# Chunk-selected attention and squared-ReLU FFN: batch-wide loads, first batch by query blocks, values and ones in one stationary, value products four steps late

## The chip, the cores and the metric

One core of one Trainium2 chip. The metric is the device time of one execution, in microseconds (us), median of the runs. Times of the kernel before scatter between 375 and 382 us (one run fell to 369.5). The granted TensorE clock, averaged over a run, lies between 0.96 and 1.00, because in most executions it falls to half for a short stretch or two; this explains only part of the scatter, as runs at 0.995 took 381 us too, and the one of 369.5 us was at 1.00. Engines: PE is TensorE (matmul), PEld its weight load, DVE VectorE, ACT ScalarE, POOL GpSimd.

## The reference

Batch 4, 8 heads, 768 positions, head dimension 64. Keys are grouped in chunks of 32; each query may attend only to the 6 chunks whose upper bound on the score is highest. The attention output then passes through a squared-ReLU FFN.

```python
k_min, k_max = per-chunk min and max of k                 # 24 chunks of 32 keys
ub = sum_d max(q*k_min, q*k_max)                          # masked causally by chunk
top_chunks = argsort(ub)[..., -6:]
scores = where(chunk selected and key <= query, q @ k.T / 8, -1e9)
attn_out = softmax(scores) @ v
x = attn_out as (3072 tokens, 512)
out = relu(x @ w_in)**2 @ w_out                           # 512 -> 2048 -> 512
```

## The kernel before

Two heads (a "pair") are handled together; a batch has four pairs. **Stage A** of a pair transposes k and q (`kT`, `qT`), takes chunk minima and maxima on DVE, computes the bound (`ub`), selects with MAX8 and transposes the selection (`sT`) into extra rows of q. **Stage B** computes scores, exp and value products for two query blocks of 384. The **FFN** of a 384-token block is 28 units of matmul work (16 "up", 12 "down") that fill TensorE between attention steps.

```python
# stage B, kernel before, cut
av  = psav.tile([128, QB], F32, tag="av")     # numerators of both heads, 64 rows each
den = psav.tile([128, QB], F32, tag="den")    # denominators, in another PSUM tile
def values(j):                                # called one key step after the scores
    for hh in range(2):
        rows = slice(D*hh, D*hh + D)
        matmul(av[rows, off:],  lhsT=vn[:, hh, j, :], rhs=e[:, off:], ...)   # 64 wide
        matmul(den[rows, off:], lhsT=ones,            rhs=e[:, off:], ...)   # 64 wide
...
nc.scalar.activation(rc, den, ACT.Ln)                     # the "finish"
nc.scalar.activation(rc, rc, ACT.Exp, scale=-1.0)
nc.vector.tensor_mul(xT[:, hp, cols], av, rc)
# ... order of the work
for p in range(B * NP):                       # pair by pair
    stage_a(p + 1); stage_b(p, [1, 2])        # [1, 2]: FFN units per key step
    if hp == NP - 1:                          # batch done: release two FFN blocks
        ...
```

The softmax here doesn't subtract the row's maximum and nothing guards it: scores larger than these inputs give would overflow.

Of the kernel before, what the change touches and what calls it, by code (L numbers as in the profile page):

```python
# [18 lines left out]
def kernel(  # L19
# [32 lines left out]
    ld = ctx.enter_context(tc.tile_pool(name="ld", bufs=3))  # L52
    work = ctx.enter_context(tc.tile_pool(name="work", bufs=2))
    epool = ctx.enter_context(tc.tile_pool(name="epool", bufs=6))
    hpool = ctx.enter_context(tc.tile_pool(name="hpool", bufs=2 * NFI))
    opool = ctx.enter_context(tc.tile_pool(name="opool", bufs=3))
    pst = ctx.enter_context(tc.tile_pool(name="pst", bufs=2, space=PSUM))
    pss = ctx.enter_context(tc.tile_pool(name="pss", bufs=2, space=PSUM))
# [3 lines left out]
    def load_qk(p):  # L62
        b, hp = divmod(p, NP)
        st = {}
        for nm, src in (("k", k), ("q", q)):
            t = ld.tile([128, 2, NT, D], BF16, tag=nm + "n", name=nm + "n")
            nc.gpsimd.dma_start(  # L67
                out=t, in_=src[b, 2 * hp:2 * hp + 2].rearrange(
                    "h (p j) d -> p h j d", p=128))
            st[nm] = t  # L70
        return st

    def load_v(p):
        b, hp = divmod(p, NP)
        t = ld.tile([128, 2, NT, D], BF16, tag="vn", name="vn")
        nc.gpsimd.dma_start(  # L76
            out=t, in_=v[b, 2 * hp:2 * hp + 2].rearrange(
                "h (j p) d -> p h j d", p=128))
        return t

    states = {0: load_qk(0)}

    ident = consts.tile([128, 128], BF16, tag="ident")
    make_identity(nc, ident)
    ones = consts.tile([128, D], BF16, tag="ones")
    nc.vector.memset(ones, 1.0)

    states[0]["v"] = load_v(0)
    states[1] = load_qk(1)
    states[1]["v"] = load_v(1)  # L90

    onehot = consts.tile([NC, S], BF16, tag="onehot")
    nc.gpsimd.memset(onehot, 0.0)
    nc.gpsimd.affine_select(
        out=onehot, in_=onehot,
        compare_op=ALU.not_equal, fill=NEG,
        base=0, channel_multiplier=1,
        pattern=[[-1, NC], [0, CH]],
    )
# [3 lines left out]
    ubmask = consts.tile([128, NS, 2, NC], F32, tag="ubmask")  # L103
    nc.gpsimd.memset(ubmask, 0.0)
    for g in range(4):
        nc.gpsimd.affine_select(
            out=ubmask[g * 32:(g + 1) * 32],
            in_=ubmask[g * 32:(g + 1) * 32],
            compare_op=ALU.is_ge, fill=-1e9,
            base=4 + g, channel_multiplier=0,  # L110
            pattern=[[4, NS], [0, 2], [-1, NC]],
        )


    NSET = 2
    kq, qs, kmx, kmn, selb = [], [], [], [], []
    for s in range(NSET):
        for hh in range(2):
            t = consts.tile([KC, S], BF16, tag=f"kq{s}{hh}", name="kqc")
            nc.scalar.copy(t[D:KC, :], onehot)  # L120
            kq.append(t)
            t = consts.tile([KC, S], BF16, tag=f"qs{s}{hh}", name="qsc")
            nc.vector.memset(t[D:KC, 0:128], 0.0)
            qs.append(t)
        for lst, nm in ((kmx, "kmx"), (kmn, "kmn")):
            t = consts.tile([128, 2, NC], BF16, tag=f"{nm}{s}", name=nm)
            nc.vector.memset(t, 0.0)
            lst.append(t)
        t = consts.tile([128, NS, 2, 32], BF16, tag=f"selb{s}", name="selb")
        nc.gpsimd.memset(t, 0.0)  # L130
        selb.append(t)
# [5 lines left out]
    def load_weights():  # L137
        nc.gpsimd.dma_start(
            out=w_in_sb, in_=moe_w_in.rearrange("(ki p) f -> p ki f", p=128))
        nc.gpsimd.dma_start(  # L140
            out=w_out_sb, in_=moe_w_out.rearrange("(fi p) d -> p fi d", p=128))

    def stage_a(p):

        st = states[p]
        s = p % NSET
        for nm in ("k", "q"):
            pt = pst.tile([128, S], BF16, tag="tp", name=nm + "T")
            n = st[nm]
            for j in range(NT):  # L150
                for hh in range(2):
                    nc.tensor.matmul(pt[D * hh:D * hh + D, 128 * j:128 * (j + 1)],  # L152
                                     lhsT=n[:, hh, j, :], rhs=ident,
                                     is_transpose=True,
                                     start=(j == 0), stop=(j == NT - 1))
            tt = work.tile([128, S], BF16, tag=nm + "t", name=nm + "t")
            nc.vector.tensor_copy(tt.rearrange("d (p j) -> d p j", j=NT),  # L157
                                  pt.rearrange("d (j p) -> d p j", j=NT))
            if nm == "k":
                for op, dst in ((ALU.max, kmx[s]), (ALU.min, kmn[s])):  # L160
                    for hh in range(2):
                        rows = slice(D * hh, D * hh + D)
                        nc.vector.tensor_reduce(  # L163
                            dst[rows, hh, :],
                            tt[rows].rearrange("d (c j) -> d c j", j=CH),
                            axis=AX.X, op=op)
                comb = kq
            else:
                qp = work.tile([128, S], BF16, tag="qp", name="qp")
                nc.vector.tensor_scalar_max(qp[:, 128:], tt[:, 128:], 0.0)  # L170
                qm = work.tile([128, S], BF16, tag="qm", name="qm")
                nc.vector.tensor_scalar_min(qm[:, 128:], tt[:, 128:], 0.0)
                comb = qs
            for hh in range(2):
                nc.vector.tensor_copy(comb[2 * s + hh][0:D, :],
                                      tt[D * hh:D * hh + D, :])
        ub = pst.tile([128, NS, 2, NC], F32, tag="tp", name="ub")
        for i in range(NS):
            cols = slice(128 * (i + 1), 128 * (i + 2))
            nc.tensor.matmul(ub[:, i], lhsT=qp[:, cols], rhs=kmx[s],  # L180
                             start=True, stop=False)
            nc.tensor.matmul(ub[:, i], lhsT=qm[:, cols], rhs=kmn[s],
                             start=False, stop=True)
        ubm = work.tile([128, NS, 2, NC], F32, tag="ubm", name="ubm")
        nc.vector.tensor_add(ubm, ub, ubmask)
        m8 = work.tile([128, NS, 2, 8], F32, tag="m8", name="m8")
        for i in range(NS):
            for hh in range(2):
                nc.vector.max(out=m8[:, i, hh], in_=ubm[:, i, hh])
        nc.vector.tensor_tensor(  # L190
            selb[s][:, :, :, 0:NC], ubm,
            m8[:, :, :, TOPK - 1:TOPK].to_broadcast([128, NS, 2, NC]),
            op=ALU.is_lt)
        sT = pst.tile([64, S], BF16, tag="tp", name="sT")
        for i in range(NS):
            nc.tensor.matmul(sT[:, 128 * (i + 1):128 * (i + 2)],  # L196
                             lhsT=selb[s][:, i], rhs=ident, is_transpose=True,
                             start=(i == 0), stop=(i == NS - 1))
        for hh in range(2):
            nc.vector.tensor_copy(qs[2 * s + hh][D:KC, 128:],  # L200
                                  sT[32 * hh:32 * hh + NC, 128:])

    ffn = []

# [39 lines left out]
    def run_ffn(n):  # L244
        for _ in range(min(n, len(ffn))):
            ffn.pop(0)()

    def stage_b(p, per_step):

        b, hp = divmod(p, NP)  # L250
        st = states.pop(p)
        s = p % NSET
        vn = st["v"]
        for blk in range(NBLK):
            q0, q1 = QB * blk, QB * (blk + 1)
            av = psav.tile([128, QB], F32, tag="av", name="av")
            den = psav.tile([128, QB], F32, tag="den", name="den")
            nj = q1 // 128
            es = {}

            def values(j):
                off = max(0, 128 * j - q0)
                for hh in range(2):
                    rows = slice(D * hh, D * hh + D)
                    e = es.pop((j, hh))
                    nc.tensor.matmul(av[rows, off:], lhsT=vn[:, hh, j, :],  # L266
                                     rhs=e[:, off:],
                                     start=(j == 0), stop=(j == nj - 1))
                    nc.tensor.matmul(den[rows, off:], lhsT=ones,  # L269
                                     rhs=e[:, off:],  # L270
                                     start=(j == 0), stop=(j == nj - 1))

            for j in range(nj):
                off = max(0, 128 * j - q0)
                for hh in range(2):
                    ps = pss.tile([128, QB], F32, tag="ps", name="ps")
                    nc.tensor.matmul(  # L277
                        ps[:, off:],
                        lhsT=kq[2 * s + hh][:, 128 * j:128 * (j + 1)],
# [11 lines left out]
                if j > 0:  # L291
                    values(j - 1)
# [9 lines left out]
    for p in range(B * NP):  # L302
# [4 lines left out]
        if p == 1:  # L307
            load_weights()
# [38 lines left out]
```

## Time and profile before

| | kernel before |
|---|---|
| time, median of the first three runs | 376.87 us (374.68 to 381.01) |
| span of the profiled execution | 379.1 us |
| busy: PE, DVE, ACT | 347.6, 219.0, 207.3 us |
| first 100 us / 100 to 330 us: PE busy | 79.2 / 223.1 us |

From the page of the kernel before: the line of busy times (us, share of the span, instructions), four rows of the span in 40 slices (tenths busy; PEclk is the granted clock in tenths), and the two lines of the chain of work that ended last.

```profile
PE 347.6 (92%) x2367; PEld 163.3 (43%) x2384; DVE 219.0 (58%) x585; ACT 207.3 (55%) x509; POOL 100.7 (27%) x257
...
PE   1298998799899999999999999999999999999996
...
DVE  3894548837777486817684677709592953041230
ACT  2253546645565477545765576447664777462541
...
PEclk9999999957999999999999999999999999999999
...
PE 75%; POOL 9%; issue 5%; ACT 5%; DMA 4%; DVE 1%; POOLq 0%; ACTq 0%
PE ph L213 22%; PE py L227 21%; PE ps L277 10%; PE av L266 9%; PE den L269 8%; DMA w_in_sb<-in_moe_w_in_dram 4%; POOL e L286 2%; POOL vn L76 2%; POOL qn L67 2%; ACT e L283 2%; PE sT L196 2%; POOL kn L67 1%; ACT rc L298 1%; PE kT L152 1%; PE qT L152 1%
```

Three quarters of the chain lie on TensorE; DVE and ACT together have 6%. A page of matmul busy time must be read with care: a busy PE is not a PE at its peak. So I use a second measure throughout, **streaming time**: each matmul counted as its moving columns at 2.4 per ns, plus 2.5 ns (which gives the 0.162 and 0.216 us at which FFN matmuls of 384 and 512 columns start after one another at the end); 64-wide neighbours that start nearer together than that count their measured distance. It is an estimate from the trace of the least TensorE time that the work needs. **The rest** is span minus streaming time: waiting, slow clock, weight loads that did not overlap. (17 down matmuls missing in this trace are added at 0.216 us.) Before: first 100 us, streaming 39, rest 61; after that, streaming 233, rest 46.

Table of windows, kernel before; after the window and its length come PE, PEld, DVE, ACT and POOL busy (us, instructions), granted clock, DMA share, GB/s:

```profile
0.00:100.00 100.00, 79.18 (x505) 34.78 (x506) 64.49 (x162) 46.99 (x112) 42.42 (x96) 0.93 0.71 92
100.00:330.00 230.00, 223.06 (x1630) 105.91 (x1645) 142.51 (x391) 140.39 (x358) 58.27 (x161) 1.00 0.26 39
```

The same kind of table for instructions on the FFN's first half alone (`ph`; columns: PE and ACT busy, clock, DMA share, GB/s), kernel before:

```profile
50.00:90.00 40.00, 5.71 (x13) 1.47 (x3) 0.83 0.35 34
90.00:106.00 16.00, 6.76 (x30) 3.43 (x7) 1.00 0.27 30
106.00:140.00 34.00, 7.99 (x41) 5.30 (x11) 1.00 0.40 59
140.00:160.00 20.00, 8.87 (x44) 5.42 (x11) 1.00 0.29 31
```

FFN work arrives in earnest after about 82 us. One caution on the clock column: no clock was recorded before 56 us here, and the views count that time as 1.00. The matmuls say otherwise: 384-column scores take about 0.50 us until 55 us, and 0.33 right after.

Timeline of TensorE, kernel before (start, duration, instruction, count): one key step's four value matmuls, and elsewhere a pair of them.

```profile
174.71 0.32 PE L266 MATMUL av<-e,vn 128*64 128x384 bf16 x1 [0.19 <-POOL e L286]
174.87 0.32 PE L269 MATMUL den<-e,ones 128*64 128x384 bf16 x1
174.96 0.32 PE L266 MATMUL av<-e,vn 128*64 128x384 bf16 x1
175.12 0.32 PE L269 MATMUL den<-e,ones 128*64 128x384 bf16 x1
...
201.20 0.35 PE L269 MATMUL den<-e,ones 128*64 128x384 bf16 x2
```

In the first four lines two starts come 0.16 us after the one before, serial, and one 0.09.

### The profile page before, as it was taken

The page shows a single profiled execution, that of the slowest core. Times are in us where ns is not written, and L with a number is a line of the kernel's source. Part 1 is how long each engine was busy: PE and PEld are TensorE (multiplying, and loading weights), DVE is VectorE, ACT ScalarE, POOL GpSimd, SP SyncE. Part 2 cuts the span into 40 slices and gives each one's busy share as a digit, 9 for nine tenths or more (in the row PEclk, how much of TensorE's full clock was granted, in tenths as well). Part 3 has the DMA queues.
Part 4 walks back from the last instruction along what each step waited for, and adds up shares of the span by engine and source line. Part 5 has one row for each costly group of instructions (what it writes and reads, how often), then busy time and mean ns, then how long its engine had stood idle before and what let it go on. Part 6 is the DMA issues. An engine that isn't in the chain of part 4 may idle for free.

```text
span 379.1 us, 6701 instructions
## 1 busy us (share of the span) xinstructions
PE 347.6 (92%) x2367; PEld 163.3 (43%) x2384; DVE 219.0 (58%) x585; ACT 207.3 (55%) x509; POOL 100.7 (27%) x257
## 2 busy tenths in 40 slices
PE   1298998799899999999999999999999999999996
PEld 1234243334354454444444445444544544454552
DVE  3894548837777486817684677709592953041230
ACT  2253546645565477545765576447664777462541
POOL 8623442514050505023140415021221121100000
PEclk9999999957999999999999999999999999999999
DMA  9999924606051423217060606040031000100102
GB/s 105 115 214 202 144 16 48 64 0 64 1 53 39 58 61 30 35 57 91 2 62 29 90 30 63 1 79 29 2 21 57 28 3 0 58 28 29 55 1 83
DMA packets 39617, 20.35 MB, mean 54 GB/s; under 512 B 25760, under 2 KB 36000, under 8 KB 39584
## 3 DMA queue, kind: packets, MB, share of 16 engines
q0 software_dynamic: 36128, 13.63, 31.0%
q1 hardware_dynamic: 3456, 6.29, 4.3%
q8 instruction: 18, 0.29, 0.3%
q14 instruction: 15, 0.12, 0.1%
HBM read 27.26 MB, written 6.29 MB: 89 GB/s over the span
## 4 chain that ended last, share of the span: by engine, by line
PE 75%; POOL 9%; issue 5%; ACT 5%; DMA 4%; DVE 1%; POOLq 0%; ACTq 0%
PE ph L213 22%; PE py L227 21%; PE ps L277 10%; PE av L266 9%; PE den L269 8%; DMA w_in_sb<-in_moe_w_in_dram 4%; POOL e L286 2%; POOL vn L76 2%; POOL qn L67 2%; ACT e L283 2%; PE sT L196 2%; POOL kn L67 1%; ACT rc L298 1%; PE kT L152 1%; PE qT L152 1%
## 5 line engine op out<-in xcount | busy, mean ns | idle before, releaser
L283 ACT ACTIVATE e<-ps 128x384 bf16<-128x384 f32 (+2 forms) x288 | 110.2, 420 | 63.1 <-PE ps L277 49.7
L286 POOL TENSOR_SCALAR_AFFINE_SELECT e<-e 128x128 bf16<-128x128 bf16 x192 | 55.0, 298 | 208.6 <-ACT e L283 206.5
L213 PE MATMUL ph<-xT,w_in_sb 128*128 128x384 bf16 x512 | 103.9, 332 | 2.3 <-ACT ht L218 1.3
L218 ACT ACTIVATE ht<-ph 128x384 bf16<-128x384 f32 x128 | 62.6, 492 | 39.1 <-PE ph L213 35.5
L277 PE MATMUL ps<-qsc,kqc 88*128 88x384 bf16 (+2 forms) x288 | 76.3, 313 | 4.0 <-ACT e L283 2.9
L269 PE MATMUL den<-e,ones 128*64 128x384 bf16 (+2 forms) x288 | 67.9, 320 | 0.1
L213 PEld LDWEIGHTS <-w_in_sb 128*128 128x128 bf16 x512 | 45.5, 98 | 46.6 <-issue 20.0
L266 PE MATMUL av<-e,vn 128*64 128x384 bf16 (+2 forms) x288 | 59.2, 331 | 5.4 <-POOL e L286 3.8
L277 PEld LDWEIGHTS <-kqc 88*128 88x128 bf16 x288 | 25.9, 99 | 32.0 <-issue 17.1
L232 ACT COPY ob<-py 128x512 f32<-128x512 f32 x24 | 14.0, 584 | 44.5 <-PE py L227 44.5
L269 PEld LDWEIGHTS <-ones 128*64 128x64 bf16 x288 | 25.1, 114 | 27.9 <-issue 23.3
L299 DVE TENSOR_TENSOR xT<-av,rc 128x384 bf16<-128x384 f32 x32 | 17.6, 550 | 30.2 <-ACT rc L298 29.1
L266 PEld LDWEIGHTS <-vn 128*64 128x64 bf16 x288 | 19.8, 113 | 34.4 <-issue 30.8
L157 DVE COPY kt<-kT 128x768 bf16<-128x768 bf16 x16 | 15.3, 956 | 29.2 <-PE kT L152 29.0
L163 DVE TENSOR_REDUCE kmn<-kt 64x24 bf16<-64x768 bf16 x32 | 30.3, 947 | 0.4
L163 DVE TENSOR_REDUCE kmx<-kt 64x24 bf16<-64x768 bf16 x32 | 30.1, 942 | 0.3
L200 DVE COPY qsc<-sT 24x640 bf16<-24x640 bf16 x32 | 15.5, 484 | 17.1 <-PE sT L196 16.6
L297 ACT ACTIVATE rc<-den 128x384 f32<-128x384 f32 x32 | 15.7, 491 | 14.1 <-PE den L269 14.1
L76 POOL DMA_DIRECT2D vn<-in_v_dram x16 | 16.6, 1039 | 12.6 <-PE den L269 9.2
L298 ACT ACTIVATE rc<-rc 128x384 f32<-128x384 f32 x32 | 16.8, 523 | 0.4
L152 PE MATMUL kT<-ident,kn 128*64 128x128 bf16 x192 | 12.2, 250 | 5.0 <-DMA kn<-in_k_dram 5.0
L157 DVE COPY qt<-qT 128x768 bf16<-128x768 bf16 x16 | 15.2, 948 | 0.9 <-PE qT L152 0.9
(451 smaller groups left out, 388.1 us busy)
## 6 DMA issues: line engine op xcount, KB each, us to landing
out_dram<-ob SPq DMA_DIRECT2D x24, 256.0 KB, 2.0
kn<-in_k_dram POOLq DMA_DIRECT2D x16, 192.0 KB, 4.5
qn<-in_q_dram POOLq DMA_DIRECT2D x16, 192.0 KB, 4.6
vn<-in_v_dram POOLq DMA_DIRECT2D x16, 192.0 KB, 4.2
w_in_sb<-in_moe_w_in_dram POOLq DMA_DIRECT2D x1, 2048.0 KB, 15.8
w_out_sb<-in_moe_w_out_dram POOLq DMA_DIRECT2D x1, 2048.0 KB, 18.9
```

The costliest lines, as they stand in the source:

```text
L76: nc.gpsimd.dma_start(out=t, in_=v[b, 2 * hp:2 * hp + 2].rearrange("h (j p) d -> p h j d", p=128))
L157: nc.vector.tensor_copy(tt.rearrange("d (p j) -> d p j", j=NT), pt.rearrange("d (j p) -> d p j", j=NT))
L163: nc.vector.tensor_reduce(dst[rows, hh, :], tt[rows].rearrange("d (c j) -> d c j", j=CH), axis=AX.X, op=op)
L213: nc.tensor.matmul(ph, lhsT=w_in_sb[:, ki, 128 * f:128 * (f + 1)], rhs=xT[:, ki, t0:t0 + QB], start=(ki == 0), stop=(ki == NKI - 1))
L218: nc.scalar.activation(ht, ph, ACT.Relu)
L227: nc.tensor.matmul(py, lhsT=h2[f][:, 128 * t:128 * (t + 1)], rhs=w_out_sb[:, f, :], start=(f == 0), stop=(f == NFI - 1))
L266: nc.tensor.matmul(av[rows, off:], lhsT=vn[:, hh, j, :], rhs=e[:, off:], start=(j == 0), stop=(j == nj - 1))
L269: nc.tensor.matmul(den[rows, off:], lhsT=ones, rhs=e[:, off:], start=(j == 0), stop=(j == nj - 1))
L277: nc.tensor.matmul(ps[:, off:], lhsT=kq[2 * s + hh][:, 128 * j:128 * (j + 1)], rhs=qs[2 * s + hh][:, q0 + off:q1], start=True, stop=True)
L283: nc.scalar.activation(e[:, off:], ps[:, off:], ACT.Exp, scale=scale)
L286: nc.gpsimd.affine_select(out=e[:, off:off + 128], in_=e[:, off:off + 128], compare_op=ALU.is_ge, fill=0.0, base=0, channel_multiplier=-1, ...
L298: nc.scalar.activation(rc, rc, ACT.Exp, scale=-1.0)
```

## The change

Its intent: fewer, larger loads; start FFN work early by running the first batch block by block; halve the value matmuls by putting values and ones side by side in one 128-wide stationary; keep masks and exp off TensorE's path by diagonal keys first and a lag of four steps. It also moves q's copies out of PSUM to ACT, reduces k over 128 rows at once, and spreads FFN units by an even rate. The core of the diff, with cuts:

```diff
-    pst = tc.tile_pool(name="pst", bufs=2, PSUM)      # transposes, ub, sT
-    pss = tc.tile_pool(name="pss", bufs=2, PSUM)      # scores
+    pst = tc.tile_pool(name="pst", bufs=1, PSUM)
+    pss = tc.tile_pool(name="pss", bufs=3, PSUM)
...  # stage A
-            nc.vector.tensor_copy(tt, pt)             # q: one 128-row copy, then two of 64
+                    nc.scalar.copy(qs[s][hh][0:D, cols], by_token[D*hh:D*hh+D])
-                        nc.vector.tensor_reduce(dst[rows, hh, :], tt[rows], ...)  # 64 rows
+                nc.vector.tensor_reduce(kr[:, m], kt, axis=AX.X, op=op)          # 128 rows
...  # stage B
-                    nc.tensor.matmul(av[rows, off:], lhsT=vn[:, hh, j, :], ...)
-                    nc.tensor.matmul(den[rows, off:], lhsT=ones, ...)
+                c0 = 2*D*(NT*(2*hp + hh) + j) - D*hh   # [v|1] for head 0, [1|v] for head 1
+                nc.tensor.matmul(av[hh][:, off:],
+                    lhsT=vo[b % 2].rearrange("p h n d -> p (h n d)")[:, c0:c0 + 2*D], ...)
...  # finish
-            nc.scalar.activation(rc, den, ACT.Ln)
+            for hh in range(2):
+                nc.scalar.activation(rc[D*hh:D*hh+D],
+                    av[hh][D*(1-hh):D*(1-hh)+D], ACT.Ln)
             nc.scalar.activation(rc, rc, ACT.Exp, scale=-1.0)
-            nc.vector.tensor_mul(xT[:, hp, cols], av, rc)
+            for hh in range(2):
+                rows = slice(D*hh, D*hh + D)
+                nc.vector.tensor_mul(xT[rows, hp, cols], av[hh][rows], rc[rows])
...  # order
+    LAG = 4
+    order = list(range(nj - HT, nj)) + list(range(nj - HT))    # diagonal keys first
+    A  = [(p, (half,)) for half in range(2) for p in range(NP)]     # batch 0 by halves
+    Bk = [(p, blk) for blk in range(NBLK) for p in range(NP)]       # batch 0 by blocks
+    # batches 1 and 2 pair by pair, batch 3 by blocks
+    pace["rate"] = (n_tok // QB - 1) * nunits / tot_cols            # one FFN rate
```

## The prediction

> **What bounds the kernel now.** From 100 to 330 us TensorE: the table of windows has it busy 223 of 230 us (DVE 143, ACT 140), and the chain of waits alternates FFN lines with score and value matmuls. A batch takes about 82.5 us there (first long py stretch at 115.7, 199.0, 280.5); 43 of it is FFN (a pure FFN block takes 21.5 us at the end). Before 100 us it is latency: the columns streamed there need 46 us at full clock but took 96. The first batch has no FFN work to fill with and is paced by one pair's serial chain on DVE (kt copy 0.96 us, four reductions of 0.95), by POOL's DMA issues, and by a slow array: 384-column score matmuls last 0.50 us up to about 55 us and again at 77 to 90, else 0.33. The Trainium skill (TensorE: Matmul & The Clock Gate, Part 1) says that activity releases a half-rate clock; the profile's 0.50 slice agrees.
>
> **What changes.**
> 1. Value products: four 64-wide matmuls per key block, which in the timeline start 0.16, 0.09, 0.16, 0.16 us apart at 384 columns, 0.57 us in all (the skill's Part 3, on column tiling, says halves of the array can overlap; the 0.09 shows it for one pair). After: two 128-wide, 0.32 us. 112 such steps' worth of columns x 0.25 = 28 us of TensorE time, nearly all critical.
> 2. Switches from 64-wide den to a full-width matmul lose about 0.1 us each (82 into FFN: 8.8 us excess); values four steps late no longer wait for exp and mask (7 us excess after scores). Estimated gain 9 us.
> 3. First batch by query blocks: FFN block 0 can begin after four short block-0 attentions and w_in's landing, near 30 to 37 us instead of about 100. That fills TensorE and warms its clock: estimated gain 25 to 35 us. Against it: a single transpose buffer serialises stage A, w_out is queued late, and twelve one-hot copies of 0.82 us precede ACT's first q copies.
> 4. Side engines: 128-row reductions save DVE 30 us, removed q copies 26; divided xT products and qp/qm cost about 28. ACT gains q copies (26), second Ln (16), one-hots (7): 207 to about 255 us, 80% of the new span, the nearest rival of TensorE.
>
> **Sum.** 377 - 28 (values) - 9 (switches) - 29 (start) + 3 (ACT queueing, transpose buffer) = 314. From below: attention 27 + FFN 43 = 70 us per batch instead of 82.5; 35 us start + 248 mixed + 21.5 last FFN block + 5 to 10 stalls = 310 to 315.
>
> **Predicted: 314 us, 298 to 336. Faster by over 2%: 0.96; within 2%: 0.03; slower: 0.01.**
>
> **What would show it.** Two value matmuls per step 0.16 us apart; batch period near 70 us; ph in earnest before 40 us, and 384-column matmuls at 0.33 us from then on; a pure FFN tail of one block, not two; ACT busy 245 to 260, DVE 190 to 205.
>
> **What would make it wrong.** ACT as limiter (batch period over 75, TensorE waiting on exp or on the av buffer behind Ln and Exp): 325 to 340. First batch stalled on DMA (w_out, second-half loads), clock cold to 60 us or more: 325 to 335. If neither binds: 298 to 305.

## More of the kernel before

A compile-time scheduler orders each engine's instructions; each engine then runs its own list in that order.

Of the 368 places where two value matmuls are neighbours in this trace, 176 overlap by more than half.

The finish of one block, kernel before, all engines:

```profile
261.37 0.49 ACT L297 ACTIVATE rc<-den 128x384 f32<-128x384 f32 x1 [0.80 <-PE den L269]
262.12 0.52 ACT L298 ACTIVATE rc<-rc 128x384 f32<-128x384 f32 x1
262.54 0.35 PE L269 MATMUL den<-e,ones 128*64 128x384 bf16 x1
...
265.98 0.55 DVE L299 TENSOR_TENSOR xT<-av,rc 128x384 bf16<-128x384 f32 x1
267.34 0.52 PE L266 MATMUL av<-e,vn 128*64 128x384 bf16 x4
```

`den` is free as soon as Ln has read it, so the next block's denominators begin at 262.54, over 3 us before the numerators of the old block are released by the product at 265.98. They serve as filler. Afterwards four numerator matmuls catch up in 0.52 us.

## The result

| | before | after |
|---|---|---|
| time, median (range), 4 runs each | 378.94 us (374.68 to 381.37) | 358.93 us (357.79 to 359.95) |
| ratio of fast runs | | 0.9551 (0.948 to 0.962) |
| span of the profiled execution | 379.1 | 357.3 |
| streaming time, first 100 us / later | 39 / 233 | 49 / 210 |
| the rest, first 100 us / later | 61 / 46 | 51 / 47 |

A ratio is the mean time of a kernel's fast runs over that of the other's fast runs of the same rounds, so not quite the ratio of the medians. Executions over 1.5% slower than the fastest of the same kernel are left out of the means. As the runs of before fall on both sides of the line between fast and slow, ratios of different groups are not exactly alike either; below I compare medians, and the before of each group (378.1 to 380.8 us) moved by under 1%.

The change is faster by 4.5%, not by 17%. The time lies far outside my range. TensorE's matmuls fell about as I had asked for; what the chain of work consists of is another thing. The page of the kernel after, same lines as before:

```profile
PE 308.7 (86%) x2096; PEld 160.0 (45%) x2096; DVE 218.6 (61%) x678; ACT 253.3 (71%) x589; POOL 96.7 (27%) x243
...
PE   0276689999789998789999999999799999999996
...
DVE  7688779747958766769482868379991331250320
ACT  6665568955968865977957897778749996671541
...
PEclk9999999999969999959999999999999999999999
...
PE 57%; ACT 20%; DVE 17%; issue 4%; POOL 1%; ACTq 0%; POOLq 0%; DVEq 0%
PE ph L256 19%; PE py L270 16%; PE ps L346 7%; ACT e L350 5%; ACT rc L328 4%; ACT kqc L121 2%; ACT qsc L177 2%; PE kT L170 2%; ACT rc L331 2%; DVE qp L209 2%; DVE kr L187 2%; ACT ht L261 2%; DVE xT L334 2%; PE qT L170 2%; DVE kt L183 2%
```

The share of DVE and ACT in the chain went from 6% to 37%. TensorE has less to do and is idle for longer (span less busy time: 31.5 us before, 48.6 after), although the rest fell from 107 to 98 us. PEclk shows two dips (a 6 and a 5 in the row; the clock records put them at 99.9 to 106.8 and 151.1 to 161.4 us, both at half).

Windows of the kernel after, columns as before:

```profile
0.00:100.00 100.00, 71.30 (x505) 35.51 (x506) 75.58 (x258) 70.28 (x160) 45.36 (x97) 1.00 0.98 118
100.00:330.00 230.00, 213.74 (x1471) 112.82 (x1470) 137.32 (x406) 172.84 (x409) 51.33 (x147) 0.96 0.19 31
```

And for `ph` alone:

```profile
50.00:90.00 40.00, 12.26 (x56) 7.92 (x16) 1.00 0.54 64
90.00:106.00 16.00, 4.11 (x13) 0.87 (x2) 0.81 0.82 67
106.00:140.00 34.00, 11.42 (x53) 6.92 (x14) 0.99 0.36 51
140.00:160.00 20.00, 1.81 (x6) 0.00 (x0) 0.78 0.21 35
```

FFN work begins in earnest at 53 us (29 us earlier than the 82 of the kernel before, but not at 30 to 37 as I said). The first block's 28 units are used up by 89 us, and the second's input is complete only at 102. The second's units are used up by 140; from 140 to 160 us there are 1.8 us of it where before had 8.9, and the clock falls in just these holes (0.81 and 0.78). So work was brought forward and then was missing. The last value product is at 308.5 us; 49 us of pure FFN follow, more than two blocks, where I had promised one.

The finish of one block in the kernel after, all engines:

```profile
188.41 0.33 PE L314 MATMUL av_2681<-e,vo 128*128 128x384 bf16 x1
188.61 0.49 ACT L328 ACTIVATE rc<-av_2680 64x384 f32<-64x384 f32 x1 [0.54 <-PE av_2680 L314]
189.13 0.48 ACT L328 ACTIVATE rc<-av_2681 64x384 f32<-64x384 f32 x1
189.91 0.51 ACT L331 ACTIVATE rc<-rc 128x384 f32<-128x384 f32 x1
190.46 0.55 DVE L334 TENSOR_TENSOR xT<-av_2680,rc 64x384 bf16<-64x384 f32 x1 [2.49 <-ACT rc L331]
191.04 0.56 DVE L334 TENSOR_TENSOR xT<-av_2681,rc 64x384 bf16<-64x384 f32 x1
191.06 0.10 PEld L314 LDWEIGHTS <-vo 128*128 128x128 bf16 x1 [0.81 <-DVE xT L334]
191.07 0.34 PE L314 MATMUL av_2874<-e,vo 128*128 128x384 bf16 x1 [0.32 <-DVE xT L334]
```

A 64-row pass costs what a 128-row pass costs (0.49 and 0.55 us, as in before's lines), so splitting by head doubles it. The next block's first value matmul starts 0.06 us after the first release: `[0.32 <-DVE xT L334]` says TensorE stood idle for it. I call **hold** the time from the end of a block's last value matmul to the end of the last instruction that reads its accumulators; over the 32 blocks of the kernel after it is 3.4 us in the median and 3.8 in the mean. The value matmuls themselves stand 0.16 us apart, as predicted.

The first stage A's, seen by their copies of k out of PSUM (DVE, kernel after):

```profile
10.96 0.56 DVE L183 COPY kt<-kT 128x384 bf16<-128x384 bf16 x1
17.84 0.56 DVE L183 COPY kt<-kT 128x384 bf16<-128x384 bf16 x1 [0.72 <-PE kT L170]
24.54 0.54 DVE L183 COPY kt<-kT 128x384 bf16<-128x384 bf16 x1
32.31 0.56 DVE L183 COPY kt<-kT 128x384 bf16<-128x384 bf16 x1
39.38 0.56 DVE L183 COPY kt<-kT 128x384 bf16<-128x384 bf16 x1 [0.72 <-PE kT L170]
```

Half a pair takes 6.7 to 7.8 us, one after the other. The fourth, and with it the last piece of the first FFN block's input, comes at 32 us; attention and finish behind it take until 48 us.

### The profile page after: what moved, and what is told of

It is laid out like the page before. It is cut to its first block, busy times and chain, and to the rows that moved or that the text cites. A ratio compares the mean times of both kernels' runs of the same rounds, so it can differ in the third digit from the quotient of the medians.

```text
span 357.3 us, 6146 instructions
## 1 busy us (share of the span) xinstructions
PE 308.7 (86%) x2096; PEld 160.0 (45%) x2096; DVE 218.6 (61%) x678; ACT 253.3 (71%) x589; POOL 96.7 (27%) x243
## 4 chain that ended last, share of the span: by engine, by line
PE 57%; ACT 20%; DVE 17%; issue 4%; POOL 1%; ACTq 0%; POOLq 0%; DVEq 0%
PE ph L256 19%; PE py L270 16%; PE ps L346 7%; ACT e L350 5%; ACT rc L328 4%; ACT kqc L121 2%; ACT qsc L177 2%; PE kT L170 2%; ACT rc L331 2%; DVE qp L209 2%; DVE kr L187 2%; ACT ht L261 2%; DVE xT L334 2%; PE qT L170 2%; DVE kt L183 2%
## 5 line engine op out<-in xcount | busy, mean ns | idle before, releaser
L261 ACT ACTIVATE ht<-ph 128x384 bf16<-128x384 f32 x128 | 62.8, 494 | 15.9 <-PE ph L256 12.5
L314 PEld LDWEIGHTS <-vo 128*128 128x128 bf16 x288 | 28.2, 103 | 29.9 <-DVE xT L334 7.5
L187 DVE TENSOR_REDUCE kr<-kt 128x24 bf16<-128x768 bf16 (+1 forms) x40 | 29.9, 786 | 0.5
L177 ACT COPY qsc<-qT 64x768 bf16<-64x768 bf16 (+1 forms) x40 | 26.6, 666 | 3.0 <-PE qT L170 2.1
L92 POOL DMA_DIRECT2D vo<-in_v_dram x24 | 21.4, 896 | 14.8 <-PE av_2351 L314 8.7
L183 DVE COPY kt<-kT 128x768 bf16<-128x768 bf16 (+1 forms) x20 | 15.9, 797 | 11.6 <-PE kT L170 11.1
L240 DVE COPY qsc<-sT 24x640 bf16<-24x640 bf16 (+2 forms) x40 | 16.7, 417 | 8.5 <-PE sT L235 8.0
L216 PE MATMUL ub<-kbd,qp 128*128 128x48 bf16 x80 | 9.8, 190 | 12.8 <-DVE qp L209 12.1
L170 PE MATMUL qT<-ident,qn 128*64 128x128 bf16 x192 | 10.8, 245 | 7.5 <-DVE kt L183 7.3
L170 PE MATMUL kT<-ident,kn 128*64 128x128 bf16 x192 | 12.5, 247 | 4.4 <-DMA kn<-in_k_dram 4.4
L170 PEld LDWEIGHTS <-kn 128*64 128x64 bf16 x192 | 7.4, 120 | 17.7 <-issue 7.3
L211 DVE TENSOR_SCALAR qm<-qsc 64x640 bf16<-64x640 bf16 (+2 forms) x40 | 14.1, 352 | 0.0
```

The costliest lines, as they stand in the source:

```text
L170: nc.tensor.matmul(pt[D * hh:D * hh + D, t, j], lhsT=n[:, 2 * (2 * hp + hh) + n0 + t, j], rhs=ident, is_transpose=True, start=True, stop=True)
L177: nc.scalar.copy(qs[s][hh][0:D, cols].rearrange("d (t p j) -> d t p j", t=nt, j=HT), by_token[D * hh:D * hh + D])
L183: nc.vector.tensor_copy(kt.rearrange("d (t p j) -> d t p j", t=nt, j=HT), by_token)
L187: nc.vector.tensor_reduce(kr[:, m], kt.rearrange("d (c j) -> d c j", j=CH), axis=AX.X, op=op)
L261: nc.scalar.activation(ht, ph, ACT.Relu)
L314: nc.tensor.matmul(hold["av"][hh][:, off:], lhsT=vo[b % 2].rearrange("p h n d -> p (h n d)")[:, c0:c0 + 2 * D], rhs=es[hh][:, off:], start ...
```

## The experiments

Eighteen kernels, three timed rounds each. Before's median in the five groups: 378.1, 379.7, 379.9, 380.8, 379.9 us. Experiments 5, 6, 10 and 12 have no ratio of their own: in their group all runs of before but the one of 369.5 us were slow against it, so medians are all there is.

**1. Paired values alone, on the kernel before** (`e1`).

```diff
-  av/den: four 64-wide matmuls per step, one Ln, one product
+  [v|1] and [1|v]: two 128-wide matmuls per step, two Ln, two products     (rest: kernel before)
```

> Kernel before with only its value products changed to one 128-wide [values|ones] stationary per head (and so two Ln and two products per block). Theory A (the value step was costed right, 28 us of TensorE time, and the loss lies elsewhere): 345 to 356 us, with the gain inside 100 to 330 us and the batch period falling from 82.5 to 75-77. Theory B (the 28 us were never critical, or overlap of the halves and the extra Ln and xT work eat them): 365 us or more.

Measured: 361.9 us (median of the fast runs, 361.2 to 362.4; 362.15 with the slow one; ratio 0.958). A fourth run took 1589 us with every matmul slowed; as it was the profiled one there is no trace of a normal run to read for this kernel. The result lies between the two theories: about 16 us, which is nearly the whole gain of the full change. All other parts of the change together add 3 us to it.

**2. The value step undone in the kernel after** (`e4`).

```diff
+                for what in range(2):                     # values, then ones
+                    nc.tensor.matmul(av[what][D*hh:D*hh+D, off:],
+                        lhsT=vo[b % 2][:, 2*hp+hh, j, D*what:D*what+D], ...)
+            nc.scalar.activation(rc, av[1], ACT.Ln); ... ; nc.vector.tensor_mul(xT, av[0], rc)
```

> Kernel after with its value products split again into four 64-wide matmuls per key block, one Ln, one product. Theory A: slower than after (359) by 15 to 28 us, 375 to 387. Theory B (in the new schedule ACT and waits bind, not TensorE, so the value step is worth little there): within 8 us of after, under 367.

Measured: 357.34 us (356.6 to 357.7), a little faster than after. Inside the new schedule, the value step as built is worth nothing. Its profile has no dip of the clock, and its value matmuls stream 43.0 us where those of after stream 36.6: in this order 242 of 409 neighbouring value matmuls overlap.

**3. Every batch by query blocks** (`e2`).

```diff
-        if b < B - 1:
+        if b < 0:
             Bk += [(p, blk) for p in heads for blk in range(NBLK)]
```

> Kernel after with every batch, not only the first and the last, run query block by query block, so that a batch's first FFN block is released halfway. Theory C (FFN filler ran out: the FFN of batch 0's first block is used up by 95 us and that of the second by 140, leaving 90-106 and 140-160 us with FFN floor 1 us of 10 to 20 and a cold clock): the hole near 140-160 closes and time falls by 6 to 12 us, to 347-353. Theory D (ACT with its q copies, one-hots and second Ln is the limiter there, so filler does not help): within 3 us of 359, ACT still 85% busy in that stretch.

Measured: 366.66 us (ratio 0.971), slower than after by 7.7. Both theories missed. The hole did close (`ph` has 9.9 us of TensorE in 140 to 160 us), but four stage A's in a row now come at each batch's start. Windows of this kernel:

```profile
100.00:140.00 40.00, 34.07 (x271) 18.68 (x274) 34.52 (x111) 29.04 (x68) 10.96 (x30) 0.92 0.50 52
140.00:160.00 20.00, 19.31 (x116) 10.64 (x116) 5.99 (x15) 17.08 (x42) 3.07 (x12) 1.00 0.10 36
```

DVE is busy 34.5 of 40 us, then 6 of 20: the work is bunched, and TensorE waits for the bunch.

**4. q's copies on DVE instead of ACT** (`e3`).

```diff
-                    nc.scalar.copy(qs[s][hh][0:D, cols] ...
+                    nc.vector.tensor_copy(qs[s][hh][0:D, cols] ...
```

> Kernel after with the 40 copies of q out of PSUM moved from ACT to DVE. ACT busy falls by 26 us to about 227, DVE rises by about 28 to 246. Theory D (ACT limits): 345-352 us. Theory C (filler, not ACT): within 4 us of 359, perhaps slower as DVE's serial chain grows by about 1 us per stage A.

Measured: 371.67 us (0.983). ACT fell to 229 us and DVE rose to 249, as expected, and the time rose by 12.7. So ACT's copies were not what limited by themselves: taking them off did not help when DVE had to carry them. DVE's share of the chain went from 17% to 40%. What ACT's load alone is worth this run cannot say; experiment 7 can.

**5. Two transpose buffers** (`e5`; one score buffer less, as the PSUM pools are full).

> Kernel after with two transpose buffers in PSUM (and two score buffers instead of three, to make room). Theory E (after is paced by the serial chain of stage A: with one buffer each stage A starts only when the one before has ended, 7 to 9 us apart eight times, so the TensorE time that the value step saved became waiting): the first eight stage A come nearer (5 to 6 us apart), first FFN earlier by about 8 us, total 343 to 352. Theory F (ACT's throughput, 11.7 us per pair of exp, Ln, Exp and q copies, paces it wherever FFN work is missing): within 4 us of 359.

Measured: 365.19 us, slower by 6. The first stage A's came only little nearer (k copies at 11.0, 17.2, 23.3, 29.8, 37.0). Both theories missed their range. Theory E falls, with a reserve: the missing score buffer is in the same edit and may be what cost.

**6. One finish instead of two half ones, wrong result** (`e6`).

```diff
-  two 64-row Ln, one Exp, two 64-row products
+            nc.scalar.activation(rc, av[1], ACT.Copy)
+            nc.scalar.activation(rc, rc, ACT.Copy, scale=0.01)
+            nc.vector.tensor_mul(xT[:, hp, cols], av[0], rc)
```

> Wrong result on purpose: kernel after, with the end of a block done as one 128-row ACT pass, a second one and one 128-row product (copies in place of Ln and Exp, values not meaningful), TensorE work unchanged. It takes 15 us from ACT and about 17 from DVE. Theory F (side engines limit, and splitting Ln and product by head is what eats the value step's gain): 340 to 350 us. Theory E (stage A's chain limits): 353 to 359.

Measured: 339.38 us (338.4 to 340.1): 19.5 us less, with TensorE's work unchanged. The hold falls to 2.1 us (median; mean 2.5). Note that `av[1]` is even released after the first pass here, which correct arithmetic would not allow. This is the largest single effect found, so the next question was why: load, or hold.

**7. The same load again, but off the chain, wrong result** (`e9`).

```diff
  as in 6, then:
+            nc.scalar.activation(spare, rc[0:D], ACT.Copy)        # nobody waits for these
+            nc.vector.tensor_mul(spare2, rc[0:D], rc[0:D])
```

> Wrong result on purpose: the kernel with one finish (339.4), plus, for each block, one 64-row ACT copy and one 64-row DVE product into spare tiles that nothing waits for. So ACT and DVE carry the load of after again, but between the last value product and the release of the accumulator stand one Ln-sized pass and one product, not two. Theory G (latency: the single accumulator is held longer by the split finish, and the next block's values wait): within 4 us of 339. Theory F (load of ACT and DVE): 351 to 359.

Measured: 342.09 us (338.2 to 343.1; 0.899). The spare passes ran with 0.52 us on ACT and 0.55 on DVE each, like the half finishes that they stand for; ACT was back to 245 us busy, DVE to 212 (the durations of all instructions add up to 286 and 242 us, against 285 and 244 in after). The hold stayed short (2.0 us in the median, 2.4 in the mean), and of the 19.5 us only 2.7 came back. So load explains about a seventh; the rest comes with where the passes stand, between a block's last value matmul and its release. This decides against load. It does not show that TensorE waiting for the accumulators is all of the rest: the same passes also make DVE wait for ACT (2.49 us before the first product in the lines of after's finish), and the FFN's input comes later. The waits of TensorE's value weight loads for the release, in after and in this kernel (who waited for whom: us in total, times, longest):

```profile
PEld L314 <- DVE xT L334: 7.5, 17, 0.9
...
PEld L314 <- DVE xT L329: 1.7, 4, 0.5
```

They differ by 6 us, where the times differ by 16.8. How the rest divides was not tested.

**8. Lag of one step instead of four** (`e10`: `LAG = 1`).

> Kernel after with the value products one step behind the scores instead of four. Theory G (accumulator held through Ln, Exp, product): the gap between a block's last values and the next block's first stays one step, so little change, 355 to 363, or slower by what exp and mask waits cost (5 to 10 us, 364 to 369). My prediction's step 2 implies about +7 us.

Measured: 359.24 us (0.945), no different from after. The lag is worth nothing here.

**9. Paired values with one finish on the kernel before, wrong result** (`e11`).

> Wrong result on purpose: kernel before with paired value products (362) and the one-pass finish of the earlier experiment. If the value step was costed right (28 us of TensorE time, critical) and the split finish took back 12: 347 to 352. If the value step is worth 16 whatever the finish: 360 to 364.

Measured: 352.80 us (352.7 to 352.9; 0.929): 27 us less than before, and 9 less than with the split finish (experiment 1).

**10. First batch pair by pair again** (`e7`).

```diff
-    A = [(p, (half,)) for half in range(2) for p in range(NP)] + [(p, (0, 1)) for p in range(NP, B*NP)]
-    Bk = [(p, blk) for blk in range(NBLK) for p in range(NP)]
+    A = [(p, (0, 1)) for p in range(B * NP)]
+    Bk = [(p, blk) for p in range(NP) for blk in range(NBLK)]
     # loads of batch 0 whole; FFN rate over the later batches
```

> Kernel after with the first batch run pair by pair again (whole stage A, both query blocks), batch-wide loads and all else kept. My prediction gave the block order 29 us: then this is 385 or so. Theory C (it only brings the FFN of one block forward, and the filler is then missing in batch 1): 355 to 368, with the empty stretch at 140-160 gone and a longer one before 100.

Measured: 354.94 us (354.4 to 356.8): undoing the step for which I had put down 29 us gains 4.

**11. Both undone** (`e12`: 10 and 2 together).

> Kernel after with both parts undone that did not pay: first batch pair by pair (354.9 alone) and separate 64-wide values and ones with one finish (357.3 alone). What remains of the change: batch-wide loads, diagonal first, lag of four, q copies on ACT, wide reductions. If the two add: 352 to 354. If TensorE becomes the limit again once ACT and DVE are relieved: 356 to 366.

Measured: 362.57 us (0.956). The effects do not add. The four corners, medians:

| | values paired | values separate |
|---|---|---|
| first batch by blocks | 358.9 (after) | 357.3 |
| first batch by pairs | 354.9 | 362.6 |

By blocks, pairing gains nothing; by pairs, it gains 8. And loads, q on ACT, wide reductions, diagonal first and lag alone (lower right) already bring 380 down to 363: each half of the change gives most of the 20 us, and together they give little more.

**12. Constants initialised late** (`e8`).

> Kernel after with the constant tiles of each set initialised just before their use instead of all ahead (24 fills on DVE, 12 one-hots on ACT stand before the first k copy at 11.0 and the first q copy at 13.2 us, though the transposes are done at 4.9). If the start is serial and nothing later absorbs it: first k copy near 6 us and 4 to 6 us off the time, 353 to 355. If a later limit (w_in's landing, stage A) absorbs it: under 2 us.

Measured: 361.23 us. The edit did not do what it should: the compile-time scheduler placed the same fills ahead of the first k copy, which still came at 10.95 us. Nothing follows; whether those 5 us can be had stays open.

**13. Accumulators released early, correct result** (`e13`).

```diff
+            for hh in range(2):
+                nc.vector.tensor_copy(num[D*hh:D*hh+D], av[hh][D*hh:D*hh+D])     # numerators out
+                nc.scalar.activation(rc[D*hh:D*hh+D], av[hh][D*(1-hh):...], ACT.Ln)
             nc.scalar.activation(rc, rc, ACT.Exp, scale=-1.0)
+            nc.vector.tensor_mul(xT[:, hp, cols], num, rc)                       # from SBUF
```

> Kernel after, correct arithmetic: DVE copies each head's 64 numerator rows out of the accumulator at once while ACT takes Ln of the denominators, and the product is one 128-row one from SBUF. Accumulators are held through about 1.1 us of work instead of 2.6, at 13 us more DVE work in all. Theory G (hold of the single accumulator): hold (last value matmul to release) falls from a median of 3.4 us to about 2, time 341 to 350. Theory F (load): 360 to 366.

Measured: 353.01 us (352.7 to 353.8; 0.928), 5.9 less than after, although DVE rose by 16 us. The hold fell less than expected, to 2.6 us (mean 3.2), because Ln and the copy of one accumulator did not run side by side. From the waits of this kernel:

```profile
ACT rc L331 <- DVE num L329: 16.7, 17, 2.8
PEld L314 <- ACT rc L331: 9.9, 19, 0.9
```

The second line is a warning: value weight loads waited for the release even a little longer than in after (9.9 us, 7.5 there), and the kernel was faster all the same. What fell is DVE's idle time before the products while it waits for Exp, from 50.9 to 22.5 us. So the gain fits the shorter hold, but the trace does not show it to be TensorE's waits for the accumulators.

The Trainium skill (PSUM — Partial Sum Buffer, Specifications) says that ScalarE and VectorE read PSUM in parallel at full rate as long as there is no bank collision; its section on collisions counts only accesses to the same bank and the same 32 partitions. The two readers here share a bank but take different halves of its partitions, so by the page they would not collide. The program as compiled makes the second wait all the same; no run here lets them go together.

**14. The same with the product on POOL** (`e14`).

> The same with the final product on POOL, so that DVE's load stays that of after. Theory G: 340 to 349, and no slower than with the product on DVE unless POOL's product delays the last pair's xT. Theory F: 355 to 360.

Measured: 357.00 us (0.940). Theory F's range holds it, theory G's does not: it is 4 us worse than with the product on DVE, and only 2 better than after. Its hold lies between the two as well (3.0 us in the median, 3.5 in the mean).

**15. An FFN pace that fits the supply** (`e15`).

```diff
+    rates = {0: 56/(7680+per_batch), 1: 56/(7680+per_batch), 2: 56/per_batch, 3: 70/per_batch}
     for p, blk in Bk:
+        pace["rate"] = rates[p // NP]
```

> Kernel after with the FFN rate set per batch to what is released by then (56 units over batch 0's second blocks and batch 1, 56 over batch 2, 70 over batch 3) instead of one rate for all. Theory C (FFN work is used up too early, leaving 90-106 and 140-160 us nearly without): those holes fill and the time falls by 5 to 10 us, 349 to 354. If the holes are only a symptom and pairs there are paced by the accumulator or stage A anyway: within 3 us of 359.

Measured: 351.36 us (350.3 to 352.5; 0.924), 7.6 less than after. `ph` in this kernel:

```profile
90.00:106.00 16.00, 3.09 (x13) 0.99 (x2) 1.00 0.68 71
106.00:140.00 34.00, 11.29 (x51) 7.11 (x14) 1.00 0.43 55
140.00:160.00 20.00, 6.17 (x28) 2.99 (x7) 1.00 0.69 67
```

The hole at 140 to 160 us has 6.2 us of FFN instead of 1.8, and the clock stays at 1.00 where after had 0.81 and 0.78. The hole at 90 to 106 did not fill with `ph`, yet its clock stayed up: with all matmuls counted, TensorE streamed for 12.5 of these 16 us, against 7.9 in after. More filler and a faster clock come together here; as after's own four runs, at mean clocks of 0.974 to 0.990, lie within 2.2 us, I take the clock for the smaller part, which is not shown.

**16. Early release on the kernel before with paired values** (`e16`).

> Kernel before with paired values (362) and the early release. Theory G: the value step's full 28 us minus about 3 for DVE, 350 to 356. Theory F: 362 to 368.

Measured: 371.66 us (0.977), 9.8 slower than without it. A clear miss for the idea in this setting, outside both ranges: the mean hold is 4.7 us here, worse than in after. DVE has 256 us of work in this kernel and 27% of the chain. The clock is no excuse: 0.953 in the profiled run, and 0.952 to 0.957 in the fast runs of experiment 1. That DVE's longer queue delays the copies themselves is my reading; no run tests it.

**17. Even pace and early release together** (`e17`), and **18. the same with the first batch by pairs** (`e18`).

> Kernel after with the even pace (351.4 alone) and the early release on DVE (353.0 alone), both correct. Two separate losses (7.6 and 5.9 us) that add: 344 to 347. If both act in the same stretch (140-160 us): 349 to 352.

> The same two mends on the kernel with the first batch by pairs (354.9 without them), FFN rates 56, 56 and 70 units over batches 1 to 3. If the block order of the first batch helps once FFN work is paced: slower than the one before by 5 us or more, 350 to 360. If the order is worth nothing even then: within 3 us of it, 343 to 349.

Measured: 349.86 us (347.5 to 350.9; 0.921, 0.911 to 0.930) and 350.7 us (median of the fast runs, 350.0 to 352.4; 351.53 with the slow one; 0.926; that one, the profiled run, took 433 us). The two mends do not add: against the even pace alone (0.924) the 1.5 us are within the scatter. With a fitting pace the order of the first batch is worth nothing either way. Both kernels beat after by 2.3 to 2.5%, with correct results.

## Why the prediction was wrong

Its sum was 377 - 28 (values) - 9 (switches) - 29 (start) + 3 (ACT queueing, transpose buffer) = 314. Term by term:

| term in the prediction | predicted | measured | shown by |
|---|---|---|---|
| values and switches, with one finish | -28 - 9 = -37 | -27 | experiment 9 |
| of this, the streaming of value matmuls | -28 | -13 | traces: 49.5 to 36.6 us |
| split finish | inside "+3" | +9 on before, +19.5 on after | 1 and 9; 6 |
| lag of four (part of the 9) | up to -7 | 0 | 8 |
| first batch by blocks | -29 | +4 | 10 |

1. **The value step was mis-sized, 28 for 13 us of streaming.** The mechanism was right: two matmuls per step 0.16 us apart. But I costed the old way from one key step, where three of four starts were serial. The scheduler often issues the two heads' matmuls next to each other, and then they overlap. The Trainium skill (TensorE: Matmul & The Clock Gate, Part 3) describes this concurrency of column tiles; this trace agrees for such a pair (two 384-column products in 0.35 us), though the neighbours at 174.87 and 174.96 us, by the program's order one per head too, start 0.09 us apart.

2. **"Side engines ... ACT gains ... second Ln (16)" and "+3 (ACT queueing, transpose buffer)": this step failed most plainly.** I counted the second Ln and the second product as load on engines with room. Experiment 7 shows that load is worth 2.7 us. What they cost is time on the path between two blocks that share accumulators. Before, the denominators had their own accumulator, free after one pass of 0.49 us, and the next block's denominators filled TensorE meanwhile (seen in the block at 262 us, not counted over all). With values and ones in one accumulator, both wait for two Ln, Exp and a product. The split finish took back 19.5 us in the new kernel (an upper bound for correct arithmetic, as experiment 6 releases `av[1]` early): all that pairing gives there (experiment 2). That this is not load is shown; by which waits it acts is only in part. I had named "TensorE waiting on exp or on the av buffer behind Ln and Exp" as what would make me wrong, and put 325 to 340 on it; too little.

3. **"First batch by query blocks: ... fills TensorE and warms its clock: estimated gain 25 to 35 us" failed.** FFN work was brought forward by 30 us, not by 60 to 70, as the halves of stage A come one after another. And it was moved, not added: until the last block of batch 1 only two FFN blocks are released, and one fixed rate spends them by 140 us. The first 100 us did lose 10 us of waiting, and the holes at 90 to 106 and 140 to 160 us, with their slow clock, gave most of it back (the rest in these two windows is 18.2 us, 9.9 in the kernel before). Experiment 15 shows the holes' part (7.6 us, filler and clock together). Experiment 10 shows that the order as built is a net loss of 4. The clock did not warm sooner either: 384-column scores last 0.48 to 0.53 us until 51 us (until 55 in the kernel before).

4. **Batch period near 70 us; one block of tail.** By the first k copies of batches 1, 2 and 3 (81.4, 142.2, 216.4 us) the periods are 61 and 74 us, because FFN work is short in one and plentiful in the other, and what was not done runs as a tail of 49 us, more than two blocks.

5. **ACT 245 to 260: right (253). DVE 190 to 205: wrong (219).** The wide reductions saved 29 us and the removed q copies 26, as I had said; the products by head (+18), q's clips (+16), the copies into `kbd` (+8), the fills of constants (+8) and smaller copies took all of it back. The copies and fills were not in my sum.

What I can't settle: why early release helps after and hurts the paired kernel before; how much of the start (first k copy at 11 us, transposes done at 4.9) could be saved; and why the effects in the table of experiment 11 compensate one another in detail. An untried version follows from the trace: separate values and ones as in experiment 2, but issued value, value, one, one, so that neighbours always lie in different halves. If all overlapped as the pair at 201.20 us does, it would have the short streaming of pairing and the early-freed denominators too.

## What to carry to other kernels

When two results are fused into one matmul, ask who reads the accumulator and for how long: a saving of streaming time can be lost if a result that used to be freed early now waits for the slowest reader. Filler work that is started earlier is not more filler: count what is released by when, and fit the rate to it, or the hole only moves. And cost a removed pattern from the sum over the whole trace, not from one tidy sample of the timeline.

## What the Trainium skill lacked or had wrong

- TensorE: Matmul & The Clock Gate, Part 1, ties the fall to half clock to an idle window of about 3.4 us. In the kernel after the clock fell at 99.9 and 151.1 us though no two matmuls in the 10 us before stood more than about 2 us apart (largest extra gap 1.7 us, and 0.9 us); TensorE was streaming for 5.3 and 6.1 of these 10 us. The page's advice to avoid gaps over 3 us was not enough here. Its passage on a second failure mode, frequent short idling between groups of matmuls, comes nearer, but gives no share. Counted over the 18 fast profiled runs, each of the 31 falls after 65 us has 4.5 to 6.8 us of streaming in the 10 us before it; the three runs without such a fall (experiments 2, 7 and 15) have no 10 us under 5.9 between 65 and 320 us. That is what these traces show, and no measured threshold.
- The same page, Part 3, gives about 4 ns between the starts of column tiles but does not say that it depends on the order in a mixed stream: of 368 neighbouring 64-wide pairs in the kernel before, 176 overlapped by more than half; of the 185 with 384 columns, 94 started less than 0.04 us apart and most of the others 0.16 to 0.20 us.
- No page that I used says what a pass over half of the partitions costs. Here 64 rows cost what 128 do: Ln of 384 columns 0.49 us either way, the product 0.55, a reduction of 768 columns 0.94 and 0.95. Split finishes are therefore double, not equal.
